# Dilated attention values in one set of matmuls, sums copied by ScalarE, and one values unit moved to a gate half

One core of one Trainium2 chip. The metric is the device time of one execution in microseconds (us), lower is better. Most executions of one kernel agree within 0.3%; every run used here is fast, with a granted clock of 0.995 to 1.0.

## The reference, cut to what matters

```python
# q, k, v: (8 batches, 8 heads, 576 tokens, 64), fp32
scores = scale * q @ k.T
rel = pos[:, None] - pos[None, :]
mask_plain = (rel >= 0) & (rel < 32)                            # heads 0 to 3
mask_dil   = (rel >= 0) & (rel < 128) & (rel % 4 == 0)          # heads 4 to 7
attn = softmax(where(mask, scores, -1e9))
x = (attn @ v).transpose(0, 2, 1, 3).reshape(4608, 512)
out = (gelu(x @ w_gate) * (x @ w_val)) @ w_out                   # 512 -> 1536 -> 512
```

A dilated head is four independent sliding windows, one for each residue of the token's position modulo 4. The kernel computes each on its own and stores the results by residue, so that somewhere they must be put back in token order.

## The kernel before

Attention is cut into 32 units of two heads each, the feed-forward block into nine stages of 512 tokens. A stage is a gate half (12 blocks of eight matmuls, each block followed by gelu on ScalarE and a product on VectorE) and an output half (48 matmuls). The scores and values of later units are slipped in between these matmuls at fixed places.

The two halves of a stage use tables of places. In `values_a` are the units whose values run in a gate half (stage: {block: unit}), in `values_b` those that run in an output half:

```python
scores   = {..., 3: range(17, 22), 4: range(22, 27), 5: range(27, 32)}
values_b = {..., 3: range(17, 20), 4: range(22, 24), 5: range(27, 28)}
values_a = {3: {4: 16}, 4: {2: 20, 6: 21}, 5: {1: 24, 4: 25, 7: 26}, 6: {1: 28, 4: 29, 7: 30, 10: 31}}
places = {...   # output half: block.position + kind (s score, m its mask, v values, x their normalization)
    4: "0.0m 1.3v 1.3s 1.3x 1.3m 2.4v 2.4s 2.4x 2.4m 2.11s 2.11m 3.7s 3.7m", ...}

for nb in range(NNB):                        # a gate half, block by block
    ...                                      # eight gate matmuls, gelu, product
    if pend is not None:
        (norm_both_x if is_plain(pend) else norm_x)(pend, SB)
        pend = None
    if nb in pv_at:
        pend = pv_at[nb]
        if is_plain(pend):
            emit_both(pend, SB)              # [v, ones, v] weights of 128 columns: values and sums in one
            norm_both_r(pend, SB)
        else:
            emit_pv(pend, SB, wide=True)     # sums (weights of ones) and values apart, 64 columns each
            norm_r(pend, SB, wide=True)
```

For a plain unit the weights are `[v, ones]` for one head and `[ones, v]` for the other, slices of one `[v, ones, v]` tile. Values then come out on 64 rows and their sums on the other 64. The normalization brings the sums to the rows of the values, in passing, by two 64-row transposes:

```python
def norm_both_r(n, b0):
    dt = nrm.tile([P, 18, 32], F32, tag="dt", bufs=1)
    for hl in range(2):
        nc.vector.transpose(dt[64 * hl : 64 * hl + 64]..., both_rows(1 - hl, b0, hl))
    recip(n, dt)                             # reciprocal, then a transpose that spreads it: rb

def norm_both_x(n, b0):                      # one multiply for each head
    for hl in range(2):
        half = slice(64 * hl, 64 * hl + 64)
        nc.vector.tensor_tensor(xT[pair(n)][half, ...], both_rows(hl, b0, hl), rb[half], ALU.mult)
```

A dilated unit's normalization in `norm_x` is one multiply of 128 rows that also reorders from residues to tokens.

The softmax here doesn't subtract the row's maximum and nothing guards it: scores larger than these inputs give would overflow.

## Time and profile before

| | before |
|---|---|
| median of three runs | 348.75 us (348.43 to 348.92) |
| profiled span | 347.0 us |
| TensorE busy | 336.0 us |
| VectorE, ScalarE, GpSimd busy | 201.8, 148.2, 84.0 us |
| stages 3 to 6, summed halves (see below) | 112.22 us |

The span is the profile's own time from first to last instruction. TensorE is busy for 97% of it, so the way to read this kernel is to look for the short stretches in which TensorE waits. I call such a stretch a **hole**: the distance between the starts of two neighbouring matmuls, less what that distance is after the same kind of matmul when nothing waits: 0.217 us for 512 columns, 0.03 to 0.07 us for the narrow matmuls of scores and values. A seam between two kinds of matmul shows as 0.09 us and is no wait.

From the same starts I take the length of each half: the gate half from its first gate matmul to the end of its last, the output half from there to the first gate matmul of the next stage. (The prediction's table cuts at the first matmul of any kind, so its lengths differ from these by up to 0.1 us.) For the kernel before, stages 3 to 6: output 15.21, gate 22.15, output 14.87, gate 22.85, output 13.55, gate 23.59.

### The profile page before, as it was taken

Reading aid. Unit: us, or ns where it says so; the run is one execution under the profiler, and the core shown is the slowest. Engines: PE = TensorE matmul, PEld = TensorE weight load, DVE = VectorE, ACT = ScalarE, POOL = GpSimd, SP = SyncE. Lnnn points to the kernel's source line nnn. Section 1 sums busy time; section 2 is a strip of 40 time slices with the busy share of each in tenths; the row PEclk is TensorE's granted clock in tenths of the full one; section 3 lists DMA queues with packets and bytes.
Section 4 is the critical chain, followed back from the end, with each engine's and each line's share of the span. In section 5 each row is a group of like instructions: output and inputs, shape, how many; then the busy total and the mean of one; then the engine's idle time right before and its main releaser. Section 6 shows DMA issues by size and latency. Waiting matters only on the chain.

```text
span 347.0 us, 6006 instructions
## 1 busy us (share of the span) xinstructions
PE 336.0 (97%) x2342; PEld 163.7 (47%) x2342; DVE 201.8 (58%) x309; ACT 148.2 (43%) x220; POOL 84.0 (24%) x123
## 2 busy tenths in 40 slices
PE   8879999999999999999999999999999999999996
PEld 3644454444544445444544454444444444444443
DVE  3784488443794359674878576975498423303320
ACT  1753473535543447336553547336633223223321
POOL 8893304630630540351006300510000000000000
PEclk9999999999999999999999999999999999999999
DMA  8999999999999999898169925991100020020002
GB/s 179 225 201 223 205 200 192 184 147 258 178 107 256 191 152 171 201 162 121 62 159 168 157 73 137 195 126 55 70 0 0 32 91 1 2 91 30 2 30 91
DMA packets 107516, 44.44 MB, mean 128 GB/s; under 512 B 83328, under 2 KB 102912, under 8 KB 107488
## 3 DMA queue, kind: packets, MB, share of 16 engines
q1 hardware_dynamic: 84192, 31.01, 39.2%
q0 software_dynamic: 22752, 12.33, 28.9%
q10 hardware_dynamic: 544, 0.72, 0.8%
q8 instruction: 18, 0.29, 0.4%
q14 instruction: 10, 0.08, 0.1%
HBM read 39.85 MB, written 9.44 MB: 142 GB/s over the span
## 4 chain that ended last, share of the span: by engine, by line
PE 70%; DVE 13%; DMA 10%; issue 3%; ACT 2%; SPq 1%; POOL 1%; DVEq 0%; POOLq 0%; ACTq 0%
PE ps L584 42%; PE ps L618 21%; PE ps L472 4%; DMA st<-in_k_dram 4%; DMA sv<-in_v_dram 3%; DMA wv<-in_moe_w_val_dram 3%; DVE dt L500 2%; DVE dt L533 2%; DVE u_all L607 2%; DVE xT L559 2%; DVE rb L544 2%; DVE P L400 2%; DVE xT L510 1%; PE ps L390 1%; DVE rc L542 1%
## 5 line engine op out<-in xcount | busy, mean ns | idle before, releaser
L607 DVE SCALAR_TENSOR_TENSOR u_all<-g,ps 128x512 f16<-128x512 f16 x108 | 72.8, 684 | 76.7 <-PE ps L584 67.9
L606 ACT ACTIVATE g<-ps 128x512 f16<-128x512 f32 x108 | 63.9, 596 | 123.3 <-PE ps L584 122.8
L584 PE MATMUL ps<-xT,wg 128*128 128x512 f16 x432 | 114.0, 379 | 1.2 <-POOL xT L707 0.7
L584 PE MATMUL ps<-xT,wv 128*128 128x512 f16 x432 | 113.8, 379 | 0.2 <-DVE u_all L607 0.2
L618 PE MATMUL ps<-wo,u_all 128*128 128x512 f16 x420 | 96.9, 380 | 0.2 <-DVE qTd L303 0.2
L584 PEld LDWEIGHTS <-wv 128*128 128x128 f16 x432 | 42.2, 98 | 52.8 <-issue 2.9
L584 PEld LDWEIGHTS <-wg 128*128 128x128 f16 x432 | 41.3, 98 | 48.9 <-issue 1.1
L618 PEld LDWEIGHTS <-u_all 128*128 128x128 f16 x420 | 38.4, 98 | 44.7 <-issue 0.8
L629 ACT ACTIVATE osb<-ps 128x512 f32<-128x512 f32 x33 | 19.7, 597 | 38.8 <-PE ps L618 37.8
L228 POOL CAST qp<-st 128x2048 f16<-128x2048 f32 x6 | 11.4, 1893 | 97.8 <-DMA st<-in_k_dram 64.8
L544 DVE STREAM_TRANSPOSE rb<-rc 128x576 f32<-128x576 f32 (+4 forms) x34 | 25.3, 743 | 1.3
L533 DVE STREAM_TRANSPOSE dt<-ps 128x576 f32<-128x576 f32 x21 | 16.3, 778 | 12.4 <-PE ps L472 12.3
L392 ACT ACTIVATE P<-ps 128x1152 f16<-128x1152 f32 x16 | 18.1, 1130 | 11.8 <-PE ps L390 11.8
L370 ACT ACTIVATE P<-ps 128x960 f16<-128x960 f32 x16 | 15.5, 970 | 11.0 <-PE ps L360 11.0
L559 DVE TENSOR_TENSOR xT<-ps,rb 128x576 f16<-128x576 f32 x16 | 17.9, 1129 | 2.2 <-PE ps L472 1.9
L400 DVE TENSOR_TENSOR P<-P,mask_d 128x1152 f16<-128x1152 f16 x13 | 9.8, 751 | 9.7 <-ACT P L392 9.7
L400 DVE TENSOR_TENSOR P<-P,mask_p 128x1344 f16<-128x1344 f16 x14 | 11.8, 856 | 2.9 <-ACT P L371 2.9
L472 PE MATMUL ps<-P,ones 128*64 128x96 f16 (+5 forms) x174 | 11.3, 244 | 2.1 <-DVE P L400 1.5
L472 PEld LDWEIGHTS <-ones 128*64 128x64 f16 x174 | 7.2, 109 | 11.5 <-issue 8.6
L631 DVE TENSOR_SCALAR osb<-ps 128x512 f32<-128x512 f32 x2 | 1.4, 691 | 18.2 <-PE ps L618 18.2
L255 POOL DMA_DIRECT2D vr<-in_v_dram x16 | 9.9, 632 | 5.3 <-DMA wv<-in_moe_w_val_dram 3.6
L500 DVE STREAM_TRANSPOSE dt<-ps 64x576 f32<-64x576 f32 x14 | 10.9, 781 | 0.4
(88 smaller groups left out, 247.8 us busy)
## 6 DMA issues: line engine op xcount, KB each, us to landing
out_dram<-osb SPq DMA_DIRECT2D x35, 256.0 KB, 2.0
sv<-in_v_dram SPq DMA_DIRECT2D x40, 128.0 KB, 3.3
st<-in_q_dram SPq DMA_DIRECT2D x24, 128.0 KB, 3.1
st<-in_k_dram SPq DMA_DIRECT2D x24, 128.0 KB, 3.1
vd<-in_v_dram POOLq DMA_DIRECT2D x7, 256.0 KB, 6.5
wo<-in_moe_w_out_dram POOLq DMA_DIRECT2D x3, 512.0 KB, 19.7
qd<-in_q_dram POOLq DMA_DIRECT2D x6, 256.0 KB, 5.4
qd<-in_k_dram POOLq DMA_DIRECT2D x6, 256.0 KB, 6.9
```

The costliest lines, as they stand in the source:

```text
L392: nc.scalar.activation(pt, ps[:, b0 : b0 + 4, 0:DW], AF.Exp, bias=0.0, scale=scale)
L400: nc.vector.tensor_tensor(pt, pt, mb, ALU.mult)
L472: nc.tensor.matmul(o, lhs, rhs, start=st, stop=True, skip_group_check=True)
L500: nc.vector.transpose(dt[64 * hl : 64 * hl + 64].rearrange("p b c -> p (b c)"), both_rows(1 - hl, b0, hl))
L533: nc.vector.transpose(dst, den)
L544: nc.vector.transpose(rb[:, 0 : 32 * nb].rearrange("p (b c) -> p b c", c=32), bass.AP(tensor=rc.tensor, offset=rc.offset, ap=[rc.ap[0], [1 ...
L559: nc.vector.tensor_tensor(dst.rearrange("p (i m s) -> p i m s", m=2, s=2), num, rb.rearrange("p (s m i) -> p i m s", s=2, m=2), ALU.mult,)
L584: nc.tensor.matmul(ps[:, bank, :], w[:, kc, ns], xT[kc][:, tok], start=first, stop=end)
L606: nc.scalar.activation(g, ps[:, banks[0], :], AF.Gelu)
L607: nc.vector.scalar_tensor_tensor(u_all[:, nb, :], g, USCALE, ps[:, banks[1], :], ALU.mult, ALU.mult)
L618: nc.tensor.matmul(ps[:, bank, :], u_all[:, fc, tb * P : (tb + 1) * P], wo_t[fc // 4][:, fc % 4, :], start=(fc == 0), stop=(fc == NNB - 1),)
L629: nc.scalar.activation(osb, ps[:, bank, :], AF.Copy, bias=0.0, scale=1.0 / USCALE)
```

## The change

Its intent: do the dilated units of batches 5 to 7 in gate halves in the `[v, ones, v]` form too, so that all 16 matmuls with 64 columns become 12 with 128. Let ScalarE copy the sums to the rows of their values, so that one VectorE transpose serves both heads. And move unit 22's values from stage 4's output half, where a second values unit made TensorE wait, to its gate half.

```diff
-    prb = ctx.enter_context(tc.tile_pool(name="prb", bufs=8))
+    prb = ctx.enter_context(tc.tile_pool(name="prb", bufs=6))
...
-            const.tile([P, HK, 4, D], F16, tag=f"vd{i}", name=f"vd{i}"),
+            const.tile([P, HP, 4, 3, D], F16, tag=f"vd{i}", name=f"vd{i}"),
...
+    values_a = {3: {4: 16}, 4: {1: 20, 4: 21, 7: 22}, 5: {1: 24, 4: 25, 7: 26}, 6: {1: 28, 4: 29, 7: 30, 10: 31}}
+    spread = (5, 6, 7)
...
+    def load_v(b, dst, src):
+        if b not in spread:
+            nc.gpsimd.dma_start(out=fl(side_by_side(dst)), in_=src)
+            return
+        for h in range(HK):
+            nc.gpsimd.dma_start(
+                out=dst[:, h // 2, :, 2 * (h % 2), :], in_=src[:, h, :].rearrange("p (r d) -> p r d", d=D)
+            )
...
+            else:                                     # emit_both, dilated
+                for s in range(2):
+                    o = ps[:, b0 + 2 * hl + s, 0:DW].rearrange("p (m i) -> p m i", m=2)
+                    src = pt[:, 2 * s + hl, :].rearrange("p (m i) -> p m i", m=2)
+                    for m in range(2):
+                        mm(o[:, m, 0:P], vd[:, hp, 2 * m + s], src[:, m, 0:P], hl, m == 0)
+                    mm(o[:, :, P:NCL], vr[:, hp, s], src[:, :, P:NCL], hl, False)
...
     def norm_both_r(n, b0):
+        dn = nrm.tile([P, S], F32, tag="dn", bufs=1)
+        for hl in range(2):
+            dst = dn[64 * hl : 64 * hl + 64]
+            if is_plain(n):
+                nc.scalar.copy(dst, both_rows(1 - hl, b0, hl))
+            else:
+                src = ps[64 - 64 * hl : 128 - 64 * hl, b0 + 2 * hl : b0 + 2 * hl + 2, 0:DW]
+                nc.scalar.copy(dst.rearrange("p (s c) -> p s c", s=2), src)
         dt = nrm.tile([P, 18, 32], F32, tag="dt", bufs=1)
-        for hl in range(2):
-            nc.vector.transpose(
-                dt[64 * hl : 64 * hl + 64].rearrange("p b c -> p (b c)"), both_rows(1 - hl, b0, hl)
-            )
+        nc.vector.transpose(dt.rearrange("p b c -> p (b c)"), dn)
...
+            else:                                     # norm_both_x, dilated
+                num = ps[half, b0 + 2 * hl : b0 + 2 * hl + 2, 0:DW].rearrange("p s (m i) -> p i m s", m=2)
+                nc.vector.tensor_tensor(
+                    dst.rearrange("p (i m s) -> p i m s", m=2, s=2),
+                    num,
+                    rb[half].rearrange("p (s m i) -> p i m s", s=2, m=2),
+                    ALU.mult,
+                )
...
-    scores = {1: range(8, 12), 2: range(12, 17), 3: range(17, 22), 4: range(22, 27), 5: range(27, 32)}
-    values_b = {1: range(8, 12), 2: range(12, 16), 3: range(17, 20), 4: range(22, 24), 5: range(27, 28)}
-    values_a = {3: {4: 16}, 4: {2: 20, 6: 21}, 5: {1: 24, 4: 25, 7: 26}, 6: {1: 28, 4: 29, 7: 30, 10: 31}}
+    scores = {1: range(8, 12), 2: range(12, 17), 3: range(17, 23), 4: range(23, 28), 5: range(28, 32)}
+    values_b = {1: range(8, 12), 2: range(12, 16), 3: range(17, 20), 4: range(23, 24), 5: range(27, 28)}
...
-        4: "0.0m 1.3v 1.3s 1.3x 1.3m 2.4v 2.4s 2.4x 2.4m 2.11s 2.11m 3.7s 3.7m",
-        5: "0.0m 1.3v 1.3s 1.3x 1.3m 2.1s 2.1m 2.10s 2.10m 3.6s 3.6m",
+        4: "0.0m 1.3v 1.3s 1.3x 1.3m 2.1s 2.1m 2.10s 2.10m 3.6s 3.6m",
+        5: "0.0m 1.3v 1.3s 1.3x 1.3m 2.3s 2.3m 3.1s 3.1m",
```

(Stage 3's places change too: the score of one more unit is put at block 0, position 8.)

## The prediction

> A **unit** is two heads of one batch (32 in all: units 0, 1 of four plain sliding-window, 2, 3 dilated, with batches 2 and 3 the other way round). A **stage** is one 512-token block: a gate half (96 matmuls of line 584), then an output half (48 of line 618). Scores and values are slipped in between.
>
> **What bounds it now.** First the busy shares and the chain by engine, to learn which engine to count:
>
> ```profile
> PE 336.0 (97%) x2342; PEld 163.7 (47%) x2342; DVE 201.8 (58%) x309; ACT 148.2 (43%) x220; POOL 84.0 (24%) x123
> ...
> PE 70%; DVE 13%; DMA 10%; issue 3%; ACT 2%; SPq 1%; POOL 1%; DVEq 0%; POOLq 0%; ACTq 0%
> ```
>
> TensorE is busy nearly always. A change pays by taking work off TensorE or by closing one of its few holes; work taken off VectorE pays only where TensorE waits for it. The matmul rate is read from an undisturbed stage in the chain, 96 matmuls in 20.80 us, so 0.217 us each. Next, the halves of stages 3 to 6, which are all that the change touches (columns: stretch, length, busy us of PE, PEld, DVE, ACT, POOL, clock, DMA share, GB/s):
>
> ```profile
> 158.79:173.90 15.11, 14.98 (x163) 7.98 (x163) 10.62 (x16) 8.99 (x12) 0.00 (x0) 1.00 0.43 88
> 173.90:196.15 22.25, 22.15 (x118) 10.47 (x117) 17.41 (x26) 9.44 (x17) 7.90 (x11) 1.00 0.90 166
> 196.15:210.93 14.78, 14.13 (x146) 7.34 (x146) 9.58 (x13) 8.77 (x11) 0.95 (x2) 1.00 0.46 89
> 210.93:233.87 22.94, 22.80 (x134) 11.09 (x133) 18.54 (x28) 9.43 (x17) 6.37 (x8) 1.00 0.97 165
> 233.87:247.40 13.53, 13.49 (x126) 6.70 (x126) 6.91 (x10) 8.91 (x11) 0.00 (x0) 1.00 0.16 59
> 247.40:271.08 23.68, 23.53 (x150) 11.68 (x149) 20.04 (x31) 9.14 (x15) 0.00 (x0) 1.00 0.04 12
> ```
>
> The odd one is the output half of stage 4, with 0.65 us of TensorE idle (14.78 - 14.13); no other of these has over 0.2. It holds two values units, and the timeline shows the second waiting for a mask that queues on VectorE behind the first one's normalization. A smaller hole of the same kind is before dilated values in a gate half (unit 26; the matmul before it leaves the array at about 225.91, so 0.31 us are lost; it waits for the normalization of unit 25, which ends at 226.16 in VectorE's timeline):
>
> ```profile
> 204.57 0.44 PE L472 MATMUL ps<-P,ones 128*64 128x192 f16 x8 [0.61 <-DVE P L400]
> ...
> 226.22 0.44 PE L472 MATMUL ps<-P,ones 128*64 128x288 f16 x4
> ```
>
> Last, the groups by form, for prices (output<-input, form, count, busy us, mean ns):
>
> ```profile
> L559 DVE TENSOR_TENSOR xT<-ps,rb 128x576 f16<-128x576 f32 x16 | 17.9, 1129 | 2.2 <-PE ps L472 1.9
> ...
> L500 DVE STREAM_TRANSPOSE dt<-ps 64x576 f32<-64x576 f32 x14 | 10.9, 781 | 0.4
> L510 DVE TENSOR_TENSOR xT<-ps,rb 64x576 f16<-64x576 f32 x14 | 10.5, 748 | 0.1
> ...
> L472 PEld LDWEIGHTS <-vd 128*64 128x64 f16 x128 | 5.5, 110 | 1.0 <-POOL vd L301 0.6 <-issue 0.4
> ...
> L485 PEld LDWEIGHTS <-vp 128*128 128x128 f16 x56 | 4.2, 98 | 1.6
> ...
> L706 ACT COPY xT<-ps 128x576 f32<-128x576 f32 x2 | 1.3, 636 | 0.0
> ```
>
> **What the Trainium skill says.** "TensorE: Matmul & The Clock Gate", section "Weight-path perf modes — Fast Weight Load (FWL) and DoubleRow": the fast load needs weights of 128 columns. The trace agrees in direction: 98 ns for 128 columns, 110 for 64. The same page, "Wait — 56ns, not 53.3ns?", gives 55.6 ns between 128-column matmuls and no less than about 25 however short. "ScalarE: Activation LUTs", "What ACT_TABLE_LOAD costs", gives 186 + 0.833 N ns, so 666 for 576 elements; the trace has 636, and I use that. "DMA: Bandwidth & Descriptors", "Specifications", says that pieces under 512 B lose rate; the new dilated loads write 128 B pieces where 512 and 256 B were written. No run here shows that size yet.
>
> **The change, part by part.** It is not chiefly a faster operation: in the old dilated values the two heads write different halves of the rows and overlap. Their four 288-column sums of unit 26 took 0.24 us (226.22 to 226.46), two columns per cycle, and all 16 matmuls took 0.63 us until the gate matmuls went on at 226.85. The new form streams 1152 columns once: 8 x 55.6 + 4 x about 27 ns (a 64-column piece in the plain form takes about 27) = 0.55 us. So 0.06 to 0.08 us per unit.
>
> For the plain units two transposes of 0.78 become two ScalarE copies of 0.64 and one transpose of about 0.78: VectorE loses 0.8 us of work per unit. But the copies start only when the values are there, so the transpose ends where the second one ended (stage 5, unit 24: both near 216.95) or 0.5 us earlier where VectorE had fallen behind (unit 25). For the dilated units VectorE gets dearer: the reordering multiply costs 1.13 us for 128 rows against 0.75 for an ordered one of 64, so its price goes by elements per row, and two of 64 rows will cost 2.26 in place of 1.13.
>
> Now by half, first without new waits:
> - Stage 3, output: one score more (0.39 us of TensorE) and a seam (0.1). +0.49.
> - Stage 4, gate: values of unit 22 come in, +0.57 with their seam; unit 20 moves to position 1, straight into a 0.26 us hole at 177.36 where TensorE waits for the first gelu. +0.31.
> - Stage 4, output: becomes what stage 5 has now (one values unit, five scores of the same kinds): 13.53 - 14.78 = -1.25.
> - Stage 5, gate: -0.06, and the 0.31 hole closes to about 0.04. -0.33.
> - Stage 5, output: one score less, -0.49.
> - Stage 6, gate: two dilated units -0.12, and the like hole before unit 30 (261.44 + 4 x 0.217 = 262.31 to 262.62) -0.27. -0.39.
>
> Sum -1.66 us. Then what I expect to be given back:
> - Stage 3: the score at position 0.8 comes 8 x 0.217 = 1.73 us after the one before it, at about 160.93; that one's exponentials end at 161.29. A wait of 0.3.
> - Stages 4 and 5: after values at position 7, taken as time 0, the copies end near 1.7, the transpose at 2.5, the reciprocal and its spread at 3.6, one product at 4.1, two multiplies at 6.4, the next product at 7.05. The last gate block's second half wants its bank at 0.57 + 3 x 1.73 + 0.87 = 6.63. 0.47 each.
> - Stage 6: unit 31 wants the rows of unit 30 at 5.77, free at 6.4. 0.55 more than now.
> - Stage 5: the score of unit 28 moves to the end of the gate half and needs the last transposed queries of batch 7; below. 0.3.
>
> At face these are 2.1 us and would leave +0.4. Each is a difference of two chains in which a few tenths decide, and the new positions look fitted to the chip; I enter them at half, 1.05. That is my choice, not a reading. Sum: -1.66 + 1.05 = -0.6, so 348.75 - 0.6 = 348.15, said as 348.2.
>
> **The rivals.** (1) Loads become the bound. Now the loads of batch 7 stand so:
>
> ```profile
> 222.83 0.77 POOL L250 DMA_DIRECT2D vd<-in_v_dram  x1
> ...
> 223.59 1.24 POOL L255 DMA_DIRECT2D vr<-in_v_dram  x2
> ...
> 225.84 6.58 SPq L284 DMA_TRANSPOSE qTp<-qp  x5
> ```
>
> Three issues taking 2.0 us become twelve: four of 0.77 and eight of about 0.57 (an issue's time hardly shrinks with its size: 0.54 for 32 KB), 7.6 us, and 1024 pieces become 3072 (counted from the rows, heads and residues that each load covers). The last transpose is issued at 231.2 and lands 2.3 us later, 233.5; unit 28 would want it at about 233.8. Against: [...]the casts that feed the transposes stand before these issues. For: the two queues share the 16 engines, whose share is 0.97 in that half. If the transposes come 3 us late the time is near 350.5. Stages 3 and 4 have margin (batch 6 lands near 196.5, wanted near 200).
> (2) VectorE or ScalarE becomes the bound in the gate halves, the face value above or twice it: 349 to 351. For: VectorE is at 20.0 of 23.7 us in stage 6. Against: the plain units give it back 0.8 each.
> (3) All waits vanish, as each exists only if two chains miss each other: 347.1.
> (4) Six buffers for probabilities instead of eight make scores wait. Against: unit n takes the buffer of n - 6; unit 28 needs 22, done in stage 4's gate half, unit 22 needs 16, done in stage 3's. No change.
>
> **Range and chances.** Rival 3 is the low end, rival 2 with a little of rival 1 the high one: 347.0 to 349.8. Two per cent is 7 us, four times all that the change can take away; only a load disaster in three stages would cost that. Faster 0.01, same 0.97, slower 0.02.
>
> **What would show it.** Right: stage 4's output half near 13.5 us with no 0.6 us wait for a mask; dilated values near 0.55 to 0.57 us; the two new multiplies near 1.13 each; VectorE's total down by about 1 us only (7 x 0.8 saved, 4 x 1.13 added), ScalarE's up by 22 x 0.64 = 14. Wrong: a multiply of 0.75 (then stages 4 to 6 gain about a microsecond more), a TensorE wait for the transposed queries at the end of stage 5's gate half, a copy that makes gelu late and TensorE wait for it in every third block, or added ScalarE table loads (the built order shows none).

## The result, and the profile after

The changed kernel took 349.0 us (median of four runs, 348.82 to 349.05), the kernel before 348.59 us (four runs, 348.35 to 348.92) in the same rounds. The ratio is 1.001, with a 95% interval of 0.9993 to 1.0027: the same time. Ratios here are the mean time of one kernel's fast runs over the mean of the other's in the same rounds, so not quite the ratio of the medians quoted.

The answer lies in the same view of stretches as in the prediction, now of the changed kernel (stretch, length, busy us of PE, PEld, DVE, ACT, POOL, clock, DMA share, GB/s):

```profile
158.80:174.53 15.73, 15.61 (x176) 8.13 (x176) 11.48 (x17) 10.17 (x13) 1.94 (x4) 1.00 0.46 89
174.53:197.74 23.21, 22.69 (x131) 11.02 (x129) 19.54 (x29) 13.77 (x22) 13.72 (x21) 1.00 1.00 159
197.74:211.19 13.45, 13.41 (x126) 6.63 (x125) 6.85 (x10) 8.24 (x11) 1.46 (x3) 1.00 0.52 104
211.19:234.38 23.19, 22.69 (x130) 11.02 (x129) 18.15 (x27) 13.75 (x22) 11.98 (x17) 1.00 1.01 160
234.38:247.69 13.31, 13.11 (x113) 6.44 (x113) 6.80 (x9) 7.23 (x10) 0.00 (x0) 1.00 0.16 60
247.69:271.21 23.52, 23.14 (x141) 11.73 (x140) 18.11 (x28) 14.21 (x23) 0.00 (x0) 1.00 0.03 12
```

The output half of stage 4 (third line) has lost its idle time: 13.45 us with 13.41 busy. But each of the three gate halves now has some: 0.52, 0.50 and 0.38 us between length and TensorE's busy time, where before they had 0.10, 0.14 and 0.15. The idle time has moved, not gone. The summed halves by my cut are 112.51 us against 112.22, so +0.29 us.

TensorE's timeline names who it waits for. These are four matmuls in these stages that stood behind a fresh wait (start, us, engine, line, operation, and in brackets the wait and its releaser):

```profile
196.78 1.02 PE L638 MATMUL ps<-xT,wv 128*128 128x512 f16 x4 [0.52 <-DVE u_all L661]
...
233.42 1.02 PE L638 MATMUL ps<-xT,wv 128*128 128x512 f16 x4 [0.50 <-DVE u_all L661]
234.98 0.20 PE L393 MATMUL ps<-qTp 64*128 64x64 f16 x2 [0.16 <-DMA qTp<-qp]
...
269.21 0.27 PE L517 MATMUL ps<-P,vd 128*128 128x128 f16 x2 [0.38 <-DVE xT L561]
```

Measured by starts, the three waits for VectorE are holes of 0.68, 0.66 and 0.53 us, and the wait for the transposed queries (qTp) is one of 0.33. (The bracket shows less after narrow matmuls, whose ends are modelled.) One more wait carries no mark: the score added to stage 3 starts its second pair of matmuls 0.32 us after the first, when ScalarE's exponentials of the score before it are done (161.30). It takes 0.67 us to the next output matmul where the same kind at 172.85 takes 0.37, so 0.30 us are lost:

```profile
161.03 0.59 PE L423 MATMUL ps<-qTd 64*128 64x128 f16 x4
...
172.85 0.28 PE L423 MATMUL ps<-qTd 64*128 64x128 f16 x4
```

Of the three holes, the first two are the last gate block of stages 4 and 5, which needs a PSUM bank that VectorE's product (L661) has yet to read. Unit 31's values wait for unit 30's rows, which the multiply (L561) has yet to read. VectorE's own timeline shows why the product is late. Unit 22's values ran on TensorE from 189.51 to 190.06:

```profile
191.34 0.78 DVE L548 STREAM_TRANSPOSE dt<-dn 128x576 f32<-128x576 f32 x1 [0.51 <-ACT dn L546]
192.15 0.27 DVE L596 RECIPROCAL rc<-dt 128x18 f32<-128x18 f32 x1
192.46 0.78 DVE L598 STREAM_TRANSPOSE rb<-rc 128x576 f32<-128x576 f32 x1
193.16 0.65 DVE L661 SCALAR_TENSOR_TENSOR u_all<-g,ps 128x512 f16<-128x512 f16 x1
193.73 2.28 DVE L561 TENSOR_TENSOR xT<-ps,rb 64x576 f16<-64x576 f32 x2
196.04 1.28 DVE L661 SCALAR_TENSOR_TENSOR u_all<-g,ps 128x512 f16<-128x512 f16 x2
```

Two multiplies take 2.28 us, and the product that TensorE is waiting for can start only at 196.04, after them. The groups by form give the prices of the new instructions, of VectorE's multiply and of ScalarE's copy of a dilated unit's sums (form, count, busy us, mean ns):

```profile
L561 DVE TENSOR_TENSOR xT<-ps,rb 64x576 f16<-64x576 f32 x8 | 9.0, 1123 | 0.1
...
L546 ACT COPY dn<-ps 64x576 f32<-64x576 f32 x8 | 5.1, 634 | 2.5 <-PE ps L517 2.3
```

In sum, VectorE's busy time fell from 201.8 to 200.7 us, ScalarE's rose from 148.2 to 162.2, and GpSimd's from 84.0 to 102.9. The chain that ended last was TensorE for 68% of the span (70% before) and VectorE for 8% (13% before).

### The profile page after: what moved, and what is told of

It reads as the page before. It is cut to its first block, busy times and chain, and to the rows that moved or that the text cites. A ratio compares the mean times of both kernels' runs of the same rounds, so it can differ in the third digit from the quotient of the medians.

```text
span 347.3 us, 6034 instructions
## 1 busy us (share of the span) xinstructions
PE 335.6 (97%) x2322; PEld 163.5 (47%) x2322; DVE 200.7 (58%) x306; ACT 162.2 (47%) x242; POOL 102.9 (30%) x156
## 3 DMA queue, kind: packets, MB, share of 16 engines
q0 software_dynamic: 29328, 12.33, 30.6%
## 4 chain that ended last, share of the span: by engine, by line
PE 68%; DMA 11%; DVE 8%; POOL 3%; issue 3%; ACT 3%; SPq 3%; POOLq 0%; DVEq 0%; ACTq 0%
PE ps L638 38%; PE ps L672 22%; DMA st<-in_k_dram 5%; DMA sv<-in_v_dram 3%; PE ps L505 3%; DMA wv<-in_moe_w_val_dram 3%; SPq L244 2%; DVE dt L587 1%; POOL vr L276 1%; PE ps L423 1%; DVE rb L598 1%; DVE P L433 1%; DVE xT L561 1%; PE ps L517 1%; DVE xT L613 1%
## 5 line engine op out<-in xcount | busy, mean ns | idle before, releaser
L661 DVE SCALAR_TENSOR_TENSOR u_all<-g,ps 128x512 f16<-128x512 f16 x108 | 72.5, 682 | 73.4 <-PE ps L638 63.2
L587 DVE STREAM_TRANSPOSE dt<-ps 128x576 f32<-128x576 f32 x17 | 13.2, 778 | 11.4 <-PE ps L505 11.1
L613 DVE TENSOR_TENSOR xT<-ps,rb 128x576 f16<-128x576 f32 x12 | 13.4, 1131 | 2.2 <-PE ps L505 1.9
L276 POOL DMA_DIRECT2D vr<-in_v_dram x24 | 14.1, 600 | 0.6 <-DMA vd<-in_v_dram 0.2
L548 DVE STREAM_TRANSPOSE dt<-dn 128x576 f32<-128x576 f32 x11 | 8.6, 778 | 6.1 <-ACT dn L543 4.6
L233 POOL CAST vp<-sv 128x1024 f16<-128x1024 f32 x8 | 8.4, 1055 | 11.4 <-DMA sv<-in_v_dram 11.4
L505 PE MATMUL ps<-P,ones 128*64 128x96 f16 (+5 forms) x154 | 9.6, 242 | 1.0 <-DVE P L433 0.8
```

The source lines that it names most:

```text
L276: nc.gpsimd.dma_start(out=dst[:, h // 2, :, 2 * (h % 2), :], in_=src[:, h, :].rearrange("p (r d) -> p r d", d=D))
L505: nc.tensor.matmul(o, lhs, rhs, start=st, stop=True, skip_group_check=True)
L587: nc.vector.transpose(dst, den)
L613: nc.vector.tensor_tensor(dst.rearrange("p (i m s) -> p i m s", m=2, s=2), num, rb.rearrange("p (s m i) -> p i m s", s=2, m=2), ALU.mult,)
L661: nc.vector.scalar_tensor_tensor(u_all[:, nb, :], g, USCALE, ps[:, banks[1], :], ALU.mult, ALU.mult)
```

## The experiments

Eleven kernels ran, all with correct results. Each is the changed kernel but for the edit shown, unless the text says otherwise. The runs of one call share a chip and the runs of the kernel before: in the first call (1 to 4) it took 348.8 us, in the second (5 to 8) 348.86, in the third (9, 10) 348.7, in the fourth 348.66, medians of 9 or 11 runs. The halves of stages 3 to 6, from the traces:

| kernel | time, us | ratio to before | out 3 | gate 4 | out 4 | gate 5 | out 5 | gate 6 | sum |
|---|---|---|---|---|---|---|---|---|---|
| before | 348.75 | | 15.21 | 22.15 | 14.87 | 22.85 | 13.55 | 23.59 | 112.22 |
| changed | 349.0 | 1.001 | 15.82 | 23.12 | 13.55 | 23.09 | 13.41 | 23.52 | 112.51 |
| 1 loads_only | 348.53 | 0.9992 | 15.21 | 22.15 | 14.88 | 22.84 | 13.55 | 23.59 | 112.22 |
| 2 copies_only | 348.75 | 0.9997 | 15.20 | 22.15 | 14.88 | 22.63 | 13.55 | 23.38 | 111.79 |
| 3 old_places | 348.95 | 1.001 | 15.20 | 22.15 | 14.87 | 23.13 | 13.55 | 23.79 | 112.69 |
| 4 order | 350.76 | 1.0054 | 15.82 | 23.74 | 13.55 | 23.72 | 13.07 | 24.16 | 114.06 |
| 5 rb_order | 350.42 | 1.0045 | 15.82 | 23.46 | 13.55 | 23.46 | 13.07 | 23.90 | 113.26 |
| 6 num_act | 348.39 | 0.9984 | 16.15 | 23.17 | 13.55 | 22.44 | 14.09 | 22.98 | 112.38 |
| 7 num_act_all | 347.41 | 0.9953 | 15.87 | 22.44 | 13.55 | 22.44 | 13.67 | 22.98 | 110.95 |
| 8 late28 | 348.6 | 1.0001 | 15.82 | 23.10 | 13.07 | 23.12 | 13.55 | 23.52 | 112.18 |
| 9 num_act_late28 | 347.44 | 0.9959 | 15.87 | 23.03 | 13.07 | 22.44 | 13.55 | 22.98 | 110.94 |
| 10 num_act_old | 347.96 | 0.9973 | 15.20 | 22.83 | 14.87 | 22.44 | 13.55 | 22.98 | 111.87 |
| 11 num_act_late28_shift | 347.17 | 0.9953 | 15.87 | 22.43 | 13.07 | 22.44 | 13.55 | 22.98 | 110.34 |

My theory after the result was that the new form of a dilated unit's normalization gives the gain back, through the two reordering multiplies. The rivals were the twelve loads in place of three, the ScalarE copies, and the new places.

### 1. Only the loads

Everything old but the `[v, ones, v]` tiles and their twelve loads in each of batches 5 to 7; the old matmuls read their `v` parts.

```diff
     def in_one(n):
-        return n in all_at and (is_plain(n) or n // NHP in spread)
+        return n in all_at and is_plain(n)
# and the old tables of places, the old two transposes in norm_both_r
```

> The kernel before with one part of the change alone: the dilated values of batches 5 to 7 lie as [v, ones, v] and are loaded by twelve small transfers per batch; the old matmuls, transposes and order read them there. Theory (waits on VectorE make up the loss, loads cost almost nothing where unit 28 is scored at its old place): within 0.2 us of before, no wait for transposed queries over 0.1 us. Rival (the loads slow the transfers or GpSimd in general): 0.4 us or more slower, with TensorE waiting for a transfer.

It took 348.53 us (five runs, 347.96 to 348.87), ratio 0.9992 with an interval of 0.998 to 1.0004. Every half is as before within 0.01 us, and no matmul waits for a load, although GpSimd was busy for 103.8 us instead of 84.0 and the number of DMA packets rose from 107516 to 114092. At the old places the loads cost nothing.

### 2. Only the copies

Only the plain units' new normalization (two ScalarE copies, one transpose); dilated values, loads and places as before.

```diff
-    spread = (5, 6, 7)
+    spread = ()
# in_one for plain units only, and the old tables of places
```

> The kernel before with the plain units' two VectorE transposes replaced by two ScalarE copies and one transpose, nothing else. Theory: the two holes of 0.31 us before the dilated values in the gate halves of stages 5 and 6 close, so 0.5 us faster than before (range 0.2 to 0.7). Rival (copies only move work that TensorE does not wait for, or make gelu late): no change, or slower.

It took 348.75 us (six runs, 347.95 to 349.25), ratio 0.9997, interval 0.9984 to 1.0009, so the times show nothing. The trace does: the holes before units 26 and 30, 0.30 and 0.31 us before, are both 0.09, a mere seam, and gate halves 5 and 6 are 0.22 and 0.21 us shorter. The copies gain 0.43 us, and this is all that the holes before the dilated values were worth.

### 3. The new forms at the old places

```diff
-    scores = {..., 3: range(17, 23), 4: range(23, 28), 5: range(28, 32)}
+    scores = {..., 3: range(17, 22), 4: range(22, 27), 5: range(27, 32)}
# and the old values_a, values_b and places
```

> The changed kernel with the old order of scores and values (unit 22 in the output half of stage 4 by the old form, units 26, 30 and 31 by the new form). Theory: the dilated form costs more on VectorE than it saves on TensorE: gate half of stage 5 about 23.2 us and of stage 6 about 23.5, with one hole of about 0.65 us before the second half of the last gate block of stage 5 and one of 0.45 within the values of unit 31; stages 3 and 4 as before; in all before + 0.1 (range -0.2 to +0.4), so copies_only + 0.6. Rival (the dilated form is a gain and only the new order loses): as fast as copies_only or faster.

It took 348.95 us (five runs, 348.75 to 349.86), ratio 1.001, interval 0.9997 to 1.0022. It differs from the kernel of experiment 2 in the dilated form alone, and gate halves 5 and 6 are 0.50 and 0.41 us longer: they have holes of 0.69 and 0.80 us (0.69 and 0.61 as the expectation counts them, for 0.65 and 0.45). So the new dilated form loses time even where nothing was moved, which clears the new places of these holes.

### 4. Another order of the multiply

The multiply walks PSUM and the reciprocals in stored order and scatters its 16-bit result instead.

```diff
-                num = ps[...].rearrange("p s (m i) -> p i m s", m=2)
+                num = ps[...].rearrange("p s (m i) -> p s m i", m=2)
                 nc.vector.tensor_tensor(
-                    dst.rearrange("p (i m s) -> p i m s", m=2, s=2), num,
-                    rb[half].rearrange("p (s m i) -> p i m s", s=2, m=2), ALU.mult)
+                    dst.rearrange("p (i m s) -> p s m i", m=2, s=2), num,
+                    rb[half].rearrange("p (s m i) -> p s m i", s=2, m=2), ALU.mult)
```

> The changed kernel with the dilated multiply of the gate halves walking PSUM in its stored order and scattering its 16-bit result instead of gathering from PSUM (same elements, loop order changed). Theory (the 1.12 us come from the order of the PSUM reads): about 0.75 us per multiply, two holes of 0.66 us and one of 0.45 us go, 1.3 to 1.7 us faster than the changed kernel, 347.3 to 347.7. Rival (the price comes from the scattered side, whichever it is, or from the number of dimensions): about 1.12 us still, no change in time.

The multiply became dearer, not cheaper. From the groups by form of this run:

```profile
L561 DVE TENSOR_TENSOR xT<-ps,rb 64x576 f16<-64x576 f32 x8 | 11.5, 1438 | 0.1
```

The idea that ordered reads would make it cheap whatever the writes do fell. But the miss settles the larger question. Each multiply is 0.315 us longer, each unit has two, and the three holes grew from 0.68, 0.66 and 0.53 to 1.31, 1.29 and 1.17 us, so by 0.63, 0.63 and 0.64 us: twice 0.315 each. The time rose to 350.76 us (five runs, 350.33 to 351.4), ratio 1.0054, interval 1.0041 to 1.0067. The pair of multiplies of units 22, 26 and 30 stands on the path that makes TensorE wait, and what it gets longer is paid there in full.

### 5. Reciprocals in token order

ScalarE's copies write the sums where their tokens are, so that the reciprocals come out in token order and the multiply reads only PSUM out of order.

```diff
-                nc.scalar.copy(dst.rearrange("p (s c) -> p s c", s=2), src)
+                nc.scalar.copy(
+                    dst.rearrange("p (i m s) -> p s m i", m=2, s=2), src.rearrange("p s (m i) -> p s m i", m=2)
+                )
...
-                    rb[half].rearrange("p (s m i) -> p i m s", s=2, m=2),
+                    rb[half].rearrange("p (i m s) -> p i m s", s=2, m=2),
```

> The changed kernel with the ScalarE copies of the dilated sums written in token order, so that the spread reciprocals come out in token order and the dilated multiply of the gate halves gathers from PSUM only. Theory (two strided reads make 1.12 us, one each for PSUM and for the reciprocals): about 0.9 to 1.0 us per multiply, and each hole of 0.67 us in stages 4 and 5 shrinks by twice the saving. Rival (the PSUM gather alone sets the price): 1.12 us still, holes as they are, time as the changed kernel. Either way the copies show what ScalarE pays for writing fp32 at a step of four elements: about 0.63 if nothing.

The groups by form of this run, again the copy of the sums and the multiply:

```profile
L546 ACT COPY dn<-ps 64x576 f32<-64x576 f32 x8 | 9.5, 1189 | 3.0 <-PE ps L517 2.9
...
L563 DVE TENSOR_TENSOR xT<-ps,rb 64x576 f16<-64x576 f32 x8 | 6.0, 748 | 0.1
```

The multiply fell to the 748 ns of an ordered one, although it still gathers from PSUM. So what made it cost 1123 was the gathered read of the reciprocals, which lie in SBUF, on top of the gathered PSUM read that both runs have. But the copies that scatter 32-bit values at a step of four elements cost 1189 ns where a plain unit's cost 632, and now the transpose waits for them: the gate halves have holes of 0.60 and 0.43, 0.59 and 0.43, and 0.60 and 0.31 us, and another of 0.5 us stands in stage 6's output half. It took 350.42 us (four runs, 350.29 to 350.78), ratio 1.0045, interval 1.003 to 1.0059. The cost moved to ScalarE and grew there.

### 6. ScalarE puts everything in order

The copies gather their reads from PSUM and write in order. ScalarE also copies the dilated numerators to a tile of 128 rows in token order, and one ordered multiply serves both heads. (For the room of that tile, five buffers of probabilities instead of six.)

```diff
-                nc.scalar.copy(dst.rearrange("p (s c) -> p s c", s=2), src)
+                nc.scalar.copy(
+                    dst.rearrange("p (i m s) -> p i m s", m=2, s=2), src.rearrange("p s (m i) -> p i m s", m=2)
+                )
...
+        nm = nrm.tile([P, S], F32, tag="nm", bufs=1)
...
-                nc.vector.tensor_tensor(dst.rearrange(...), num, rb[half].rearrange(...), ALU.mult)
+                nc.scalar.copy(nm[half].rearrange("p (i m s) -> p i m s", m=2, s=2), num)
+        nc.vector.tensor_tensor(xT[pair(n)][:, b * S : (b + 1) * S], nm, rb, ALU.mult)   # dilated units only
```

> The changed kernel with the dilated numerators of the gate halves copied by ScalarE, in token order, into one tile of 128 rows, and one ordered VectorE multiply of 128 rows in place of two reordering ones of 64 (five buffers for probabilities in place of six, for the space). Theory (the doubled multiply on VectorE makes the holes of 0.68, 0.66 and 0.34 us): the multiply falls to about 0.75 once, all three holes go to under 0.1, gate halves about 22.5, 22.5 and 23.2 us by the trace; 1.4 us faster than the changed kernel, near 347.6. Rival (any added work in the gate halves costs TensorE, ScalarE included): gelu comes late, TensorE waits for it, no gain or slower.

Gathering reads cost ScalarE nothing: 633 ns for the sums, 626 for the numerators. Gate half 5 fell from 23.09 to 22.44 us and gate half 6 from 23.52 to 22.98, neither with a hole. Gate half 4, though, has one of 0.73, and its multiply of unit 22, in VectorE's timeline, is three times as long as the other three (740 to 743 ns):

```profile
193.49 2.45 DVE L570 TENSOR_TENSOR xT<-nm,rb 128x576 f16<-128x576 f32 x1
```

GpSimd's timeline in that stretch has its casts of the values:

```profile
193.95 1.05 POOL L233 CAST vp<-sv 128x1024 f16<-128x1024 f32 x1
194.92 0.41 POOL L237 CAST vt<-sv 128x256 f16<-128x256 f32 x1
195.27 1.15 POOL L297 COPY kTr<-qTd 128x512 f16<-128x512 f16 x1
```

The last of them takes 1.15 us where the changed kernel had 0.61. The Trainium skill, "SBUF — State Buffer", section "Who interferes with whom", says that a VectorE instruction with two inputs in SBUF contends with a GpSimd instruction that reads SBUF, and that one with at most one SBUF input does not, outside certain fast modes. That fits: this multiply has two SBUF inputs (the copied numerators and the reciprocals), while in the changed kernel one input came from PSUM, and its mean stayed at 1123 ns beside the same casts. Experiment 11 tests the collision; the second SBUF input as its reason was not tested apart. Two output halves were also longer than in the changed kernel, stage 5's by 0.68 us, where the early score now waits about 1.0 us in all for its transposed queries, and stage 3's by 0.33, with a hole of 0.32 just before the gate half. The time was 348.39 us (six runs, 347.45 to 349.25), ratio 0.9984, interval 0.997 to 0.9998, short of the 347.6 us expected.

### 7. The same for plain units

```diff
-        by_act = not is_plain(n)
+        by_act = True
```

> As num_act, for the plain units of the gate halves too. Theory: by then TensorE waits for nothing there, so no further gain: gate halves as in num_act within 0.1 us, VectorE about 5 us less busy, ScalarE about 9 us more. Rival (VectorE's length still matters in the gate halves): a further 0.3 us or more faster. If ScalarE gets too full: holes with TensorE waiting for gelu.

It took 347.41 us (five runs, 346.84 to 347.51), ratio 0.9953, interval 0.9941 to 0.9965. The three gate halves in the view of stretches:

```profile
174.02:196.45 22.43, 22.43 (x129) 10.89 (x127) 16.37 (x26) 16.53 (x28) 12.76 (x20) 1.00 1.02 165
...
210.00:232.44 22.44, 22.44 (x129) 10.93 (x129) 15.05 (x24) 16.52 (x28) 11.99 (x17) 1.00 1.10 165
...
246.11:269.09 22.98, 22.98 (x142) 11.65 (x141) 14.99 (x24) 17.64 (x30) 0.00 (x0) 1.00 0.03 12
```

Length and TensorE's busy time are equal: no hole is left in a gate half. VectorE's busy time fell to 189.5 us and ScalarE's rose to 174.8. All eleven multiplies cost 741 ns; the one of unit 22 ran from 193.08 to 193.82 here and the casts began at 193.71, so that the two met for 0.1 us at most. Gate halves 5 and 6 are as in experiment 6, as expected, but the expectation of no further gain fell: 0.73 us more are gained in gate half 4, where the collision was missed, and 0.70 in output halves 3 and 5, where the waits are shorter. Why they are was not tested. By the ratios to the kernel before, this kernel beats both.

### 8. Unit 28's score back to where it was

The changed kernel, with the score of unit 28 at block 1, position 3 of stage 5's output half again, where the transposed queries have long been there.

```diff
-    scores = {..., 4: range(23, 28), 5: range(28, 32)}
+    scores = {..., 4: range(23, 27), 5: range(27, 32)}
-        4: "0.0m 1.3v 1.3s 1.3x 1.3m 2.1s 2.1m 2.10s 2.10m 3.6s 3.6m",
-        5: "0.0m 1.3v 1.3s 1.3x 1.3m 2.3s 2.3m 3.1s 3.1m",
+        4: "0.0m 1.3v 1.3s 1.3x 1.3m 2.3s 2.3m 3.1s 3.1m",
+        5: "0.0m 1.3v 1.3s 1.3x 1.3m 2.1s 2.1m 2.10s 2.10m 3.6s 3.6m",
```

> The changed kernel with the score of unit 28 moved back to position 1.3 of stage 5 (unit 27 at its end of the gate half again, one score less in stage 4, one more in stage 5). Theory: the wait for the transposed queries of batch 7 at the end of stage 5's gate half goes (0.16 us more than a seam), the rest only moves from stage 4 to stage 5: 0.1 to 0.3 us faster than the changed kernel, inside the noise of the times, so read from the trace. Rival (the transfers hold stage 5 up more than the wait shows): 0.5 us or more faster.

It took 348.6 us (four runs, 348.23 to 350.39), ratio 1.0001, interval 0.998 to 1.0022. Output halves 4 and 5 together are 26.62 us instead of 26.96, so the early score cost 0.34 us, while the three holes in the gate halves stayed at 0.67, 0.68 and 0.53 us. No run scores unit 28 early with the old loads, so how much of the 0.34 us is due to the loads is open.

### 9. Experiments 7 and 8 together

```diff
# num_act_all, with the tables of late28
```

> num_act_all with unit 28 scored at its old place (position 1.3 of stage 5). Theory: its two remedies add up: the waits for transposed queries go (0.3 us by the sum of the output halves in late28), 347.1, ratio to before about 0.9945. Rival (with the gate half shorter, the score at its end comes so early that its wait was larger, so more is gained; or the order of stage 4 needs the extra score): under 346.9, or no gain over num_act_all.

It took 347.44 us (five runs, 346.81 to 347.55), ratio 0.9959, interval 0.9946 to 0.9971, no better than experiment 7 and short of the 347.1 us expected. The two output halves gained 0.60 us against it, and gate half 4 lost 0.59: now the casts begin at 193.46, and unit 22's multiply meets them.

```profile
193.68 2.36 DVE L570 TENSOR_TENSOR xT<-nm,rb 128x576 f16<-128x576 f32 x1
```

### 10. Experiment 7 at the old places

```diff
# num_act_all, with scores, values_b, values_a and places of the kernel before
```

> num_act_all with the old order of scores and values (unit 22 in the output half of stage 4 by the old form). It tells what moving unit 22 is worth once the gate halves have no holes. Theory, from the halves measured so far (stage 3 output 15.2, stage 4 22.15 and 14.87, stage 5 22.45 and 13.55, stage 6 22.98): sum of the six 111.2 against 110.95 of num_act_all, so 0.25 us slower than it, 347.65. Rival (the move is the point of the change, and gains what the output half of stage 4 lost, 1.3 us): 348.4 or more.

It took 347.96 us (five runs, 347.47 to 348.6), ratio 0.9973, interval 0.9959 to 0.9986. Here another multiply, at 183.73, took 2.46 us while GpSimd cast the queries and keys, and made a hole of 0.68 us. By the sums, moving unit 22 is worth 111.87 - 110.95 = 0.92 us; without that hole, 0.24 us. Most of what the move seems to bring beside the new normalization is luck with the collision.

### 11. The casts moved

Experiment 9, with GpSimd's cast of the values between the two groups of its load issues instead of after them. No wait is taken away: only GpSimd's order changes.

```diff
     def load_v_dil(b):
         load_v(b, tiles["v", b][1], quads(v, b, HK, 0, 4 * P))
+        if b in spread:
+            v_cast(b, tiles["plain", b][1])
         load_v_dil_rest(b)
...
-        v_cast(b, sv)
+        if b not in spread:
+            v_cast(b, sv)
```

> The kernel num_act_late28 with one thing moved: in batches 5 to 7 GpSimd's cast of the values stands between the vd issues and the vr issues instead of after them, so that its casts fall at another time than VectorE's multiply of unit 22. Theory (the slow multiplies are VectorE instructions with two SBUF inputs that meet GpSimd casts): no multiply of form 128x576 over 0.9 us (before: one of 2.36), the 0.59 us hole of stage 4's gate half goes and that half is 22.45 instead of 23.03, stages 3 to 6 sum to about 0.5 us less than in num_act_late28, and the time is about 0.4 us below num_act_all, 347.0. Rival (something else makes that one multiply slow, or the casts, once moved, meet another multiply): a multiply of 2.3 us or more stays somewhere, the half stays at 23.0 or another gate half becomes 23.0, and the time stays at 347.4.

The casts of that batch now begin at 189.27, and unit 22's multiply is normal again:

```profile
193.62 0.74 DVE L573 TENSOR_TENSOR xT<-nm,rb 128x576 f16<-128x576 f32 x1
```

Gate half 4 is 22.43 us instead of 23.03, the sum of the halves 110.34 instead of 110.94, the lowest of all. The theory of the collision holds. One part of the expectation missed: three other multiplies are slower than 0.9 us (1.54 us at 150.13, beside casts at 150.01 to 151.94; 1.03 at 187.89 and 0.95 at 223.40, beside GpSimd's load issues and no recorded cast). None of the three made a hole. Why the last two are slow is open; the issues alone don't explain it, as multiplies beside the same issues took 0.74 us in experiments 7 (at 187.34) and 9 (at 187.94). The 0.30 us wait of stage 3's added score is still there too; no run moved that score alone. The time was 347.17 us (five runs, 346.8 to 347.42), ratio 0.9953, interval 0.9939 to 0.9967. That is not told apart from experiment 7 by the times, as the ratios are equal; by the halves it is 0.6 us better.

## Why the prediction was right or wrong

The class, same, and the range were right, but the point was not: it said 0.6 us faster, and the changed kernel was 0.35 us slower by the ratio, with an interval that includes no change. That the class held says little, as 2% would be 7 us. The time came out 0.8 us above the point and 0.8 below the upper end. By its own steps:

- **Stage 4's output half becomes what stage 5 had**: right, -1.32 us for -1.25, and the wait for a mask of 0.77 us (by starts) is gone.
- **Stage 4's gate half, +0.31, with unit 20 falling into the 0.26 hole, and 0.47 given back**: the hole is filled; the half is 0.97 us longer instead of 0.78.
- **Stage 5's gate half, -0.33 + 0.47**: +0.24 us for +0.14.
- **Stage 6's gate half, -0.39 + 0.55**: -0.07 for +0.16. The wait of unit 31 came as entered, 0.53 us for 0.55, but more was gained than -0.39: -0.60 without the wait. In the new form no seam is left beside the values: unit 31's took 0.73 us from gate matmul to gate matmul before and take 0.55 in experiment 7, where nothing waits.
- **Output halves**: stage 3 +0.61 for +0.49 + 0.3. The wait is there, 0.30 us; the half is shorter than the sum in part because two holes before values, of 0.18 and 0.27 us, shrank to seams, while one of 0.18 arose inside the second dilated unit's sums. Stage 5 -0.14 for -0.49 + 0.3: the wait measured 0.33, and experiment 8 put the price of the early score at 0.34 us.
- **"I enter them at half, 1.05"** is the step that failed. The five waits were taken at half on the ground that each could vanish and that the places looked fitted to the chip. All five came, about as large as at face value or larger: 0.30, 0.68, 0.66, 0.53 and 0.33 us, 2.5 in all for 2.1. The halves add to +0.29 us, where the face value would have given 2.1 - 1.66 = +0.4 and half gave -0.6. That +0.4 comes so near is partly luck: the gains without waits were larger too, 2.2 us for 1.66, and the two misses cancel. The worked chain for unit 22 gave no ground for doubt: it put the copies' end at 1.7, the transpose at 2.5, the spread at 3.6, one product at 4.1, the multiplies at 6.4 and the next product at 7.05 us after the values began. From the trace (less 189.51) they are 1.80, 2.61, 3.73, 4.30, 6.50 and about 7.2. The wait was then 0.68 where 0.47 was entered (its own figures, 7.05 - 6.63, give 0.42). Experiment 4, where holes follow the multiply to 0.01 us, shows that there was no slack to absorb any of it.
- **Rival 1, the loads**: it fell, by experiment 1, but for the 0.33 us wait in stage 5, in which the loads may have a part (experiment 8). **Rival 2**, VectorE in the gate halves at face value, is what happened, though VectorE was not full there (19.54 of 23.21 us in stage 4): its chain came late. **Rival 3**, no waits, did not happen. Experiment 11 has no wait left in a gate half and took 347.17 us for the 347.1 named there, but it is another kernel and stage 3's wait of 0.30 us is still in it, so this is no test of that sum.
- **Rival 4, six buffers of probabilities**: no wait for one was seen, and five served experiments 6, 7 and 9 to 11, of which 11 has no hole in a gate half.
- **Prices**: the multiply 1123 ns for 1.13, the copy 634 for 636, dilated values 0.55 us for 0.55, VectorE -1.1 us for about -1, ScalarE +14.0 for 14. The sentence that the multiply's "price goes by elements per row" was too simple: its price is half again that of an ordered one because it gathers from SBUF (experiment 5).

What the change left undone is the two multiplies. With the numerators copied by ScalarE as well (experiment 7), VectorE needs one multiply of 0.74 us in place of two of 1.12, and the same layout and places are 0.47% faster than before.

## What to carry to other kernels

When a chain of waits has been worked out from measured durations and comes out positive, enter it whole: here the chain of an engine that is not the bottleneck, ending late on a PSUM bank that TensorE wanted, was paid to the tenth of a microsecond. Reorder data with an engine whose gathered reads cost nothing extra (633 ns against 634) and whose time is idle, here ScalarE reading PSUM, and leave the loaded engine one instruction over all 128 rows. And when a multiply is given a second SBUF input, look where GpSimd's casts fall beside it.

## What the Trainium skill lacked or had wrong

- "SBUF — State Buffer", section "Who interferes with whom": its rule on two SBUF inputs agrees. Here a 0.74 us multiply took 2.36 to 2.46 us in three runs beside GpSimd casts, and a GpSimd copy 1.15 for 0.61. The page's summary says that the second of the two to issue blocks until the first finishes. In experiment 6 it was not so by the trace, where GpSimd's times are rough: the multiply began first (193.49, the cast 193.95) and was still the one held up. That descriptor generation spares such a multiply is only inferred there; beside load issues it took 0.74 us in experiments 7 and 9, but 1.03 and 0.95 in 11.
- "SBUF — State Buffer", section "Door 1: The DMA port swizzle (why `[64,N]` ≈ `[32,N]`)": it speaks of 16-byte lines and of strides that are free up to 8 elements of 16 bits or 4 of 32 bits. VectorE's 16-bit writes at a step of four elements were not free: 1438 ns (experiment 4) for 748 when ordered. ScalarE's 32-bit writes at a step of four elements were not either: 1189 ns for 632 (experiment 5).
- The same place says of PSUM that access patterns out of order slow matmuls; it has nothing on other engines' reads. Gathered PSUM reads were free for ScalarE (633 and 633 ns) and for VectorE (748 and 748 ns).
- "VectorE: DVE Perf Modes", section "Mode 1× (REGULAR) — the baseline": it says that odd strides work and gives no price (the note on 16-byte lines says only that there is one). A gathered read of the 32-bit SBUF operand, with PSUM gathered in both, took the multiply from 748 to 1123 ns.
- "ScalarE: Activation LUTs", section "What ACT_TABLE_LOAD costs": its formula gives 666 ns for 576 elements; the copies here took 634.
- "DMA: Bandwidth & Descriptors", section "Specifications": pieces under 512 B are said to lose rate. With 6576 packets more and 128 B pieces no time was lost (experiment 1, ratio 0.9992). The packets of GpSimd's queue took 30.7% of the DMA engines' span instead of 28.9 for the same 12.33 MB; that is all that the runs show of the loss.
